# A Fourier mixing layer with a gated channel MLP: a chunk's two products exchanged in the middle of two passes, and the last chunks' loads and splits put elsewhere

## The chip, the cores and the metric

The kernel runs on one core of one Trainium2 chip. The metric is the device time of the whole program in microseconds (us), the median of several runs. TensorE (PE in the profile) multiplies; its weight loads are shown apart, as PEld. VectorE (DVE) and ScalarE (ACT) do elementwise work, GpSimd (POOL) and SyncE (SP) mostly issue DMAs here.

## The reference

`x` is 2048 x 512. It is layer-normalised to `xn`; `s` is the real part of a two-dimensional DFT of `xn`, written as matrix products; `g` is a channel MLP of `xn` behind SiLU.

```python
a = jnp.einsum("bsd,ed->bse", x, dft_hid_re)
b = jnp.einsum("bsd,ed->bse", x, dft_hid_im)
y = jnp.einsum("ts,bse->bte", dft_seq_re, a) - jnp.einsum("ts,bse->bte", dft_seq_im, b)
...
y = _layernorm(x, axis=-1)
h = _gelu(jnp.einsum("bsd,df->bsf", y, w1) + b1)
return jnp.einsum("bsf,fd->bsd", h, w2) + b2
...
xn = _layernorm(x, axis=-1)
s = _A_ref(xn, A_dft_seq_re, A_dft_seq_im, A_dft_hid_re, A_dft_hid_im)
g = _silu(_B_ref(xn, B_w1, B_b1, B_w2, B_b2))
return x + s * g
```

## The kernel before

All products keep float32 accuracy by splitting each operand into a high and a low half: ScalarE rounds it (`h` in the names, L64), VectorE subtracts the rounded value (`l`, L65). A product is then three matmuls, high by high, high by low, low by high. Seven products replace eight in each of the three large matrix multiplications.

The stages follow each other on TensorE: the hidden DFT (accumulators `pd`), the MLP's first half (`hx`, `hy`, `hz`), its second half (`ma`, `mb`), and then the sequence DFT, which the change touches. That one runs over 16 chunks `n` of 128 rows of the 2048 x 2048 matrices `ct`, each 128 x 1024 (512 KB), in passes `q`, listed in `passes`:

- Pass 0 multiplies `s4` (accumulators `px`) and `s3` (`pz`).
- Pass 1 multiplies `s2` (`pz`) and `a1` (`px`).
- Pass 2 goes on in the same accumulators with `b2` (`pz`) and `b1` (`px`); chunks 8 to 11 (`DEFER`) do only `b2`.
- Pass 3 multiplies `s1` (`pw`). Its last four chunks (`LAST`) are done in four *pieces* of 12 matmuls, one for each half of columns (`tau`) and of rows (`k`), so that the results can be finished piece by piece. Pieces 1 and 3 share the accumulator tile `pw30`, pieces 2 and 4 `pw31`.
- Pass 4 does the deferred `b1` of chunks 8 to 11, also in four pieces, into `px`.

In a product the chunk's split operand (`R_..h`, `R_..l`) is multiplied with a split left operand (`L_nh`, `L_nl`), which serves two chunks. `multiply_by` issues for each half of rows and columns (lh, rh), (lh, rl), (ll, rh): the second matmul is the first to need the chunk's low half, the third the first to need the left operand's. A product of a chunk has 12 matmuls.

A *unit* is one chunk of one pass. `ahead("load")`, `ahead("sum")` and `ahead("split")` run a few units ahead of the products, and their calls set the order on every queue: nothing is reordered later. `unit_load` issues the loads on SP; `unit_sum` forms the sums (L786, L791, L797); `unit_split` splits the left operand and the chunk. In pass 2 `unit_sum` splits `b1` first, then adds the held sum `t` to the raw chunk to make `b2` (L791), and `unit_split` splits that. At the end of a pass `evacuate` (L690) lets ScalarE copy the accumulators.

Places: the pool `op` has 39 places of 512 KB tiles for split operands, held sums and guests (`guest`); the pool `lp` (`room`) has 7 such places for raw loads. A load waits on SP until the place that it takes is free, and SP issues in order.

After each piece of pass 3, `end` issues on VectorE two multiplications with the gates (L999), which read the accumulator, and two additions (L1000), one of each for the two outputs that share `pw`, and SP stores the results (L1001). After a piece of pass 4 there is one of each; the addition reads `px`, a tile loaded at L964 with part of the input.

Of the kernel before, what the change touches and what calls it, by code (L numbers as in the profile page):

```python
# [22 lines left out]
def fnet_mixer_kernel(ctx: ExitStack, tc: tile.TileContext, x, xT, ct, wt, w1, w2, b1, b2, out):  # L23
# [3 lines left out]
    NS = S // P  # L27
# [7 lines left out]
    op = ctx.enter_context(tc.tile_pool(name="op", bufs=39))  # L35
# [6 lines left out]
    lp = early.enter_context(tc.tile_pool(name="lpa", bufs=4))  # L42
# [10 lines left out]
    def guest(name):  # L53
        return op.tile([P, 2, W], F32, tag="op", name=name)
# [4 lines left out]
    def room(name):  # L59
        return lp.tile([P, 2, W], F32, tag="l", name=name)  # L60
# [362 lines left out]
    for i in range(3, NS):  # L423
# [11 lines left out]
        if i == 4:  # L435
# [5 lines left out]
            lp = early.enter_context(tc.tile_pool(name="lpm", bufs=2, reuse_waits="tile"))  # L441
# [233 lines left out]
    def banks(name):  # L675
        return [acc_two(f"{name}{k}") for k in range(2)]

    def multiply_by(acc, left, right, first, last):
        (lh, ll), (rh, rl) = left, right
        for k in range(2):  # L680
            for tau in range(2):
                terms = [(lh[k], rh), (lh[k], rl), (ll[k], rh)]
                for i, (a, c) in enumerate(terms):
                    nc.tensor.matmul(acc[k][:, tau, :], a, c[:, tau, :], start=first and i == 0,  # L684
                                     stop=last and i == len(terms) - 1, skip_group_check=True)

    def evacuate(acc, name):
        out_ = [guest(f"{name}{k}") for k in range(2)]
        for k in range(2):
            nc.scalar.activation(out_[k], acc[k], AF.Copy)  # L690
        return out_
# [49 lines left out]
    def left(name, i):  # L741
        if name[0] == "s":
            return s_d[int(name[1]), i].rearrange("p (c e) -> p c e", c=2)
        e = int(name[1]) - 1
        return (a_d if name[0] == "a" else b_d)[i][:, :, e * W2:(e + 1) * W2].rearrange("c p e -> p c e")

    passes = [("s4", "s3"), ("s2", "a1"), ("b2", "b1"), ("s1",), ("b1",)]
    DEFER = (8, 9, 10, 11)  # L750
    units = [(q, n) for q in range(4) for n in range(NS)] + [(4, n) for n in DEFER]
    c_raw, c_left, c_ops, t_hold = {}, {}, {}, {}

    def names(q, n):
        return ("b2",) if q == 2 and n in DEFER else passes[q]

    at = {"load": 0, "sum": 0, "split": 0}

    def c_in(key, src, where):
        t = (guest if where == "op" else room)(f"{key}")  # L760
        nc.sync.dma_start(out=t, in_=src)
        return t

    def unit_load(u):
        q, n = units[u]
        if n % 2 == 0:
            t = room(f"la{q}_{n}")
            for v, name in enumerate(names(q, n)):
                nc.sync.dma_start(out=t[:, v, :].rearrange("p (c e) -> p c e", c=2), in_=left(name, n // 2))
            c_left[q, n // 2] = t  # L770
        if q == 0:
            c_raw[u] = {"s4": c_in(f"c22_{n}", ct[1, 1, n], "lp")}
            t_hold[n] = c_in(f"c12_{n}", ct[0, 1, n], "op")
        elif q == 1:
            c_raw[u] = {"a1": c_in(f"c11_{n}", ct[0, 0, n], "lp")}
        elif q in (2, 4):
            c_raw[u] = {"b1": c_in(f"c21_{q}_{n}", ct[1, 0, n], "lp")}
        elif n % 2:
            c_raw[u] = {"s1": c_in(f"d22_{n}", ct[1, 1, n], "lp")}

# [36 lines left out]
    def ahead(what, until):  # L817
        while at[what] < min(len(units), until):
            {"load": unit_load, "sum": unit_sum, "split": unit_split}[what](at[what])
            at[what] += 1  # L820
# [40 lines left out]
    for u, (p, j) in enumerate(m_units):  # L861
# [3 lines left out]
        if u == 1:  # L865

            n = NJ - 1
            h_product(n, 4)
            early.close()
            lp = early.enter_context(tc.tile_pool(name="lp", bufs=7, reuse_waits="tile"))  # L870
            gp = early.enter_context(tc.tile_pool(name="gp", bufs=4, reuse_waits="tile"))
            m_at["room"] = 1
        n = NJ - 1
# [9 lines left out]
        q = m_order.index(p)  # L883
# [23 lines left out]
    def factors(u, name):  # L907
        q, n = units[u]
        lr = [[t[:, (n % 2) * W2 + k * P:(n % 2) * W2 + (k + 1) * P] for k in range(2)] for t in c_left[q, n // 2][name]]
        return lr, c_ops[u][name]  # L910
# [7 lines left out]
    def gate_load(e, h):  # L918
        for k in range(2):
            gate[e, h, k] = gp.tile([P, 2, W], F32, tag="g", name=f"zr{e}{h}{k}") if h else guest(f"zr{e}{h}{k}")  # L920
            nc.sync.dma_start(out=gate[e, h, k], in_=z_d[h, 2 * e + k])

    def gate_open(e, h):
        for k in range(2):
            nc.scalar.activation(gate[e, h, k], gate[e, h, k], AF.Silu, bias=b2_t[:, 2 * e + k:2 * e + k + 1])

    def gated(e, h, k, src, dst):
        nc.vector.tensor_mul(dst, src, gate[e, h, k])
        nc.gpsimd.dma_start(out=dst, in_=xT[2 * h:2 * h + 2, 2 * e + k].rearrange("b p w -> p b w"), accum_op=ALU.add)

    def put_out(e, h, k, src):
        kk = 2 * e + k
        nc.gpsimd.dma_start(out=out[kk * P:(kk + 1) * P, 2 * h * W:2 * (h + 1) * W],
                            in_=src.rearrange("p b w -> p (b w)"))
# [8 lines left out]
    def after(q, n):  # L943
        for k in range(2):
            if (q, n) == (2, 1 + k):
                nc.vector.tensor_add(part["3", k], part["3", k], part["1", k])
                nc.vector.tensor_add(part["7", k], part["7", k], part["1", k])
            if (q, n) == (2, 3 + 2 * k):
                nc.vector.tensor_add(part["3", k], part["3", k], part["6", k])
            if (q, n) == (2, 4 + 2 * k):  # L950
                nc.vector.tensor_add(part["6", k], part["6", k], part["7", k])
            if (q, n) == (2, 8 + k):
                gated(0, 1, k, part["3", k], part["3", k])
            if (q, n) == (2, 10 + k):
                gated(1, 1, k, part["6", k], part["6", k])
            if (q, n) == (3, 1):
                nc.vector.tensor_add(part["7", k], part["7", k], part["8", k])
            if (q, n) == (3, 5):
                gated(1, 0, k, part["7", k], part["7", k])
            if (q, n) == (3, 8):  # L960
                put_out(1, 0, k, part["7", k])
            if (q, n) == (3, 9):
                part["x", k] = guest(f"px{k}")
                nc.sync.dma_start(out=part["x", k], in_=xT[0:2, k].rearrange("b p w -> p b w"))  # L964
        if (q, n) in GATES:
            gate_load(*GATES[q, n])
        if (q, n - 3) in GATES:
            gate_open(*GATES[q, n - 3])

    for u, (q, n) in enumerate(units):  # L970
        lead = 6 if q > 2 else 1 if q == 1 and n > 13 or q == 2 and n < 4 else 2
        ahead("load", u + lead + 4)
        ahead("sum", u + lead + 2)
        ahead("split", u + lead + 1)
        if n == 0:
            for name in passes[q] if q != 2 else ():
                acc[KEY[name]] = banks(f"p{KEY[name]}{q}")
        if q < 3 or q == 3 and n < NS - LAST:
            for name in names(q, n):
                multiply_by(acc[KEY[name]], *factors(u, name), n == 0 and q != 2, n == NS - 1 and name not in ("s2", "a1", "b1"))  # L980
                if n == NS - 1 and name in COPY:
                    for k, t in enumerate(evacuate(acc[KEY[name]], "p" + COPY[name])):
                        part[COPY[name], k] = t
        if u == 0:
            m_after(7)
        after(q, n)
# [3 lines left out]
    def piece(name, us, tau, k):  # L990
        for u in us:
            (lh, ll), (rh, rl) = factors(u, name)
            for i, (a, c) in enumerate([(lh, rh), (lh, rl), (ll, rh)]):
                nc.tensor.matmul(acc[KEY[name]][k][:, tau, :], a[k], c[:, tau, :], start=False,  # L994
                                 stop=u == us[-1] and i == 2, skip_group_check=True)
# [8 lines left out]
    for tau in range(2):  # L1004
        for k in range(2):
            piece("s1", [4 * NS - LAST + i for i in range(LAST)], tau, k)
            for do in zip(end(0, 1, k, tau, "w", "3"), end(1, 1, k, tau, "w", "6")):
                for o in do:
                    o()
    for tau in range(2):  # L1010
        for k in range(2):
            piece("b1", range(4 * NS, len(units)), tau, k)
            for o in end(0, 0, k, tau, "x", "x"):
                o()
# [33 lines left out]
```

## Time and profile before

| | |
|---|---|
| median of 3 runs | 680.47 us (680.40 to 682.38) |
| profiled execution, its time | 683.88 us |
| profiled execution, its span | 682.1 us |
| mean granted TensorE clock | 0.996 |
| VectorE busy | 538.3 us |
| DMA over the span | 171.49 MB, mean 251 GB/s |

The span is the time from the first to the last instruction. In the views, a group or row names the line, the engine, the operation and output<-inputs; a time in square brackets is idle time of the engine just before, with what ended it. The timeline has the start and the length of each instruction, with x for how many were joined. A table by stage has, for each stretch, the busy time of each engine with its count of instructions, then PEclk, the clock that TensorE was granted (1.00 is full), the busy share of the DMA engines, and GB/s. Matmuls overlap: a row of 0.39 us is followed by the next start 0.23 us later.

### The profile page before, as it was taken

How to read it: one execution, taken by the hardware profiler on the slowest of the kernel's cores; microseconds unless marked ns; L12 is line 12 of the kernel's file. 1: busy time of each engine (PE TensorE's matmuls, PEld its weight loads, DVE VectorE, ACT ScalarE, POOL GpSimd, SP SyncE). 2: the span in 40 equal slices, each digit the busy share in tenths (PEclk: the TensorE clock that was granted, in tenths of full speed). 3: DMA queues.
4: the chain of work that ended last, by engine and by line, in shares of the span. 5: the costliest groups of instructions: out<-in, count | busy, mean ns of one | idle time of the engine just before them, and what ended most of it. 6: DMA issues, size and time to landing. Idle time of an engine off the chain costs nothing.

```text
span 682.1 us, 8179 instructions
## 1 busy us (share of the span) xinstructions
PE 668.9 (98%) x2933; PEld 548.3 (80%) x2933; DVE 538.3 (79%) x595; ACT 347.8 (51%) x366; POOL 47.0 (7%) x80
## 2 busy tenths in 40 slices
PE   8999999999999999999999999999999999999986
PEld 5888888888888888888888888888888877888865
DVE  6877887877777864788979998649686399999975
ACT  4443566544545665555455554364456544637720
POOL 1000000212122100000000000000000000210100
PEclk9999999999999999999999999999999999999989
DMA  8666731899989997688799996325455279996953
GB/s 295 217 233 225 266 136 57 301 345 326 331 323 326 417 374 301 227 311 278 263 387 407 364 327 231 117 80 185 155 189 151 67 194 250 289 296 219 266 209 124
DMA packets 69897, 171.49 MB, mean 251 GB/s; under 512 B 6593, under 2 KB 20961, under 8 KB 69857
## 3 DMA queue, kind: packets, MB, share of 16 engines
q1 hardware_dynamic: 58304, 132.67, 55.9%
q0 software_dynamic: 11200, 37.76, 17.3%
q10 hardware_dynamic: 352, 0.54, 0.3%
q8 instruction: 23, 0.38, 0.2%
q14 instruction: 18, 0.14, 0.1%
HBM read 120.60 MB, written 50.35 MB: 251 GB/s over the span
## 4 chain that ended last, share of the span: by engine, by line
PE 92%; DMA 3%; DVE 3%; issue 1%; ACT 0%; SPq 0%; DVEq 0%; ACTq 0%
PE pz L684 18%; PE px L684 16%; PE pd L305 12%; PE ma L684 11%; PE hy L518 11%; PE mb L684 8%; PE hz L518 6%; PE pw L684 4%; PE hx L518 3%; DMA c<-ct 2%; PE px L994 2%; DMA rw<-wt 1%; PE pw L994 1%; DVE R_b2l L65 1%; DVE W L279 0%
## 5 line engine op out<-in xcount | busy, mean ns | idle before, releaser
L786 DVE TENSOR_TENSOR c<-c,c 128x1024 f32<-128x1024 f32 x32 | 39.0, 1218 | 3.5 <-DMA c<-ct 3.5
L65 DVE TENSOR_TENSOR w1l<-w1r,w1h 128x1792 fp32r<-128x1792 f32 x7 | 14.2, 2025 | 24.5 <-ACT w1h L64 24.5
L65 DVE TENSOR_TENSOR R_b1l<-c,R_b1h 128x1024 fp32r<-128x1024 f32 x16 | 19.4, 1220 | 16.8 <-ACT R_b1h L64 16.8
L305 PE MATMUL pd<-W,xt_0h 128*128 128x512 f32 x96 | 29.8, 392 | 0.0
L64 ACT ACTIVATE R_b2h<-c 128x1024 fp32r<-128x1024 f32 x16 | 17.0, 1060 | 25.1 <-DVE c L791 20.0
L684 PE MATMUL pw<-R_s1h,L 128*128 128x512 f32 x96 | 29.7, 389 | 0.0
L305 PE MATMUL pd<-W,xt_1h 128*128 128x512 f32 x96 | 29.6, 389 | 0.0
L64 ACT ACTIVATE R_s3h<-c 128x1024 fp32r<-128x1024 f32 x16 | 17.0, 1061 | 24.4 <-DVE c L786 16.1
L65 DVE TENSOR_TENSOR R_a1l<-c,R_a1h 128x1024 fp32r<-128x1024 f32 x16 | 19.6, 1222 | 10.3 <-PE px L684 8.0
L523 ACT ACTIVATE hc<-hc,b_t 128x1024 f32<-128x1024 f32 x14 | 16.2, 1154 | 20.3 <-DVE hc L558 19.7
L64 ACT ACTIVATE R_s2h<-c 128x1024 fp32r<-128x1024 f32 x16 | 16.9, 1059 | 16.9 <-PE px L684 15.2
L65 DVE TENSOR_TENSOR R_s2l<-c,R_s2h 128x1024 fp32r<-128x1024 f32 x16 | 19.5, 1221 | 5.4 <-PE pz L684 5.0
L64 ACT ACTIVATE R_b1h<-c 128x1024 fp32r<-128x1024 f32 x16 | 16.7, 1053 | 12.7 <-DMA c<-ct 8.7
L64 ACT ACTIVATE R_a1h<-c 128x1024 fp32r<-128x1024 f32 x16 | 16.9, 1056 | 12.3 <-PE pz L684 8.7
L65 DVE TENSOR_TENSOR R_s3l<-c,R_s3h 128x1024 fp32r<-128x1024 f32 x16 | 19.5, 1218 | 3.8 <-PE pz L684 3.8
L64 ACT ACTIVATE R_s1h<-c 128x1024 fp32r<-128x1024 f32 x16 | 16.4, 1052 | 11.3 <-DVE c L797 11.3
L684 PEld LDWEIGHTS pw<-R_s1h,L 128*128 128x128 f32 x96 | 18.0, 188 | 3.8
L305 PEld LDWEIGHTS pd<-W,xt_1h 128*128 128x128 f32 x96 | 18.0, 188 | 3.8
L305 PEld LDWEIGHTS pd<-W,xt_0h 128*128 128x128 f32 x96 | 17.8, 188 | 4.0
L794 POOL DMA_DIRECT2D c<-ct x8 | 6.9, 868 | 203.2 <-ACT R_a1h L64 144.8
L791 DVE TENSOR_TENSOR c<-c,c 128x1024 f32<-128x1024 f32 x16 | 19.6, 1223 | 0.4
L65 DVE TENSOR_TENSOR R_s4l<-c,R_s4h 128x1024 fp32r<-128x1024 f32 x16 | 19.5, 1217 | 0.4 <-PE px L684 0.4
(886 smaller groups left out, 2177.1 us busy)
## 6 DMA issues: line engine op xcount, KB each, us to landing
c<-ct SPq DMA_DIRECT2D x68, 512.0 KB, 5.9
m<-h_d SPq DMA_DIRECT2D x48, 512.0 KB, 6.6
h_d<-ht POOLq DMA_DIRECT2D x21, 512.0 KB, 7.2
s_d<-sa SPq DMA_DIRECT2D x32, 256.0 KB, 4.0
la<-s_d SPq DMA_DIRECT2D x32, 256.0 KB, 6.0
h_d<-hc POOLq DMA_DIRECT2D x13, 512.0 KB, 3.8
x<-x SPq DMA_DIRECT2D x16, 256.0 KB, 5.4
xT<-xT SPq DMA_DIRECT2D x8, 512.0 KB, 7.0
```

The costliest lines, as they stand in the source:

```text
L64: nc.scalar.activation(hi, src, AF.Copy)
L65: nc.vector.tensor_sub(lo, src, hi.bitcast(F32))
L305: nc.tensor.matmul(acc, xt[i, k][px], weights[m * NK + k][pw], start=n == 0, stop=n == len(terms) - 1)
L518: nc.tensor.matmul(acc[:, tau, :], w[:, W1_AT[p], k * P:(k + 1) * P], r[:, k, :], start=p in (1, 5, 2) and i == 0, stop=p in (2, 3, 4) and ...
L523: nc.scalar.activation(dst, src, AF.Gelu_apprx_tanh, bias=b1_t[:, row:row + 1])
L684: nc.tensor.matmul(acc[k][:, tau, :], a, c[:, tau, :], start=first and i == 0, stop=last and i == len(terms) - 1, skip_group_check=True)
L786: nc.vector.tensor_sub(t, t, raw)
L791: nc.vector.tensor_add(raw, raw, t)
L794: nc.gpsimd.dma_start(out=t, in_=ct[1, 1, n], accum_op=ALU.add)
L994: nc.tensor.matmul(acc[KEY[name]][k][:, tau, :], a[k], c[:, tau, :], start=False, stop=u == us[-1] and i == 2, skip_group_check=True)
```

## The change

Nothing is added to or taken from the computation: the same products, sums, splits, loads and stores are issued. Four things move.

1. `passes` names the two products of passes 1 and 2 the other way round, so that the product on `px` comes first in the middle of both passes. `in_order` turns them back for chunk 0 of pass 1 and chunk 15 of pass 2. The splits and the halves of the left operand follow `names`, so they are turned in all of pass 1.
2. The raw chunks of pass 4 (`c_4_8` to `c_4_11`) are loaded into places of `op` instead of `lp`.
3. `px` is loaded at chunk 12 of pass 3 instead of chunk 9.
4. The splits of the last two units (chunks 10 and 11 of pass 4, with their left operand) are issued after the `end` of pass 3's first piece, and not before the pieces.

```diff
-    passes = [("s4", "s3"), ("s2", "a1"), ("b2", "b1"), ("s1",), ("b1",)]
+    passes = [("s4", "s3"), ("a1", "s2"), ("b1", "b2"), ("s1",), ("b1",)]
...
+    def in_order(q, n):
+        return names(q, n)[::-1 if (q, n) in ((1, 0), (2, NS - 1)) else 1]
...
         elif q in (2, 4):
-            c_raw[u] = {"b1": c_in(f"c21_{q}_{n}", ct[1, 0, n], "lp")}
+            c_raw[u] = {"b1": c_in(f"c21_{q}_{n}", ct[1, 0, n], "lp" if q == 2 else "op")}
...
-            if (q, n) == (3, 9):
+            if (q, n) == (3, 12):
                 part["x", k] = guest(f"px{k}")
...
-        ahead("split", u + lead + 1)
+        ahead("split", min(u + lead + 1, 4 * NS + 2))
         if n == 0:
-            for name in passes[q] if q != 2 else ():
+            for name in in_order(q, n) if q != 2 else ():
                 acc[KEY[name]] = banks(f"p{KEY[name]}{q}")
         if q < 3 or q == 3 and n < NS - LAST:
-            for name in names(q, n):
+            for name in in_order(q, n):
...
             for do in zip(end(0, 1, k, tau, "w", "3"), end(1, 1, k, tau, "w", "6")):
                 for o in do:
                     o()
+            ahead("split", len(units))
```

TensorE in pass 2, where chunk 4 ends and chunk 5 begins, before:

```order
L684 MATMUL px_3812<-R_4_b1h,L_4h 128x512
L684 MATMUL px_3812<-R_4_b1l,L_4h 128x512
L684 MATMUL px_3812<-R_4_b1h,L_4l 128x512
L684 MATMUL pz_3809<-R_5_b2h,L_4h 128x512
L684 MATMUL pz_3809<-R_5_b2l,L_4h 128x512
L684 MATMUL pz_3809<-R_5_b2h,L_4l 128x512
```

The same place in the changed program:

```order
L684 MATMUL pz_3810<-R_4_b2h,L_4h 128x512
L684 MATMUL pz_3810<-R_4_b2l,L_4h 128x512
L684 MATMUL pz_3810<-R_4_b2h,L_4l 128x512
L684 MATMUL px_3811<-R_5_b1h,L_4h 128x512
L684 MATMUL px_3811<-R_5_b1l,L_4h 128x512
L684 MATMUL px_3811<-R_5_b1h,L_4l 128x512
```

Chunk 5 now begins with `b1`, and `b2` comes as the second product of its chunk.

VectorE at the pieces of pass 3, before (`R_8` to `R_11` here are the chunks of pass 4, `zr` the gates, `pw_5032` and `pw_5033` the two accumulators):

```order
L65 TENSOR_TENSOR R_9_b1l<-c_4_9_5202,R_9_b1h 128x1024
L65 TENSOR_TENSOR L_10_5289<-la_10_5226,L_10_5289 128x512
L65 TENSOR_TENSOR R_10_b1l<-c_4_10_5228,R_10_b1h 128x1024
L65 TENSOR_TENSOR R_11_b1l<-c_4_11_5252,R_11_b1h 128x1024
L999 TENSOR_TENSOR zr_4222<-pw_5032,zr_4222 128x512
L999 TENSOR_TENSOR zr_4634<-pw_5032,zr_4634 128x512
L1000 TENSOR_TENSOR zr_4222<-zr_4222,p_3774 128x512
L1000 TENSOR_TENSOR zr_4634<-zr_4634,p_4399 128x512
L999 TENSOR_TENSOR zr_4224<-pw_5033,zr_4224 128x512
L999 TENSOR_TENSOR zr_4636<-pw_5033,zr_4636 128x512
```

The same place in the changed program, whose lines 1003 and 1004 are 999 and 1000 of before:

```order
L65 TENSOR_TENSOR R_9_b1l<-c_4_9_5202,R_9_b1h 128x1024
L1003 TENSOR_TENSOR zr_4222<-pw_5032,zr_4222 128x512
L1003 TENSOR_TENSOR zr_4634<-pw_5032,zr_4634 128x512
L1004 TENSOR_TENSOR zr_4222<-zr_4222,p_3774 128x512
L1004 TENSOR_TENSOR zr_4634<-zr_4634,p_4415 128x512
L65 TENSOR_TENSOR L_10_5307<-la_10_5226,L_10_5307 128x512
L65 TENSOR_TENSOR R_10_b1l<-c_4_10_5228,R_10_b1h 128x1024
L65 TENSOR_TENSOR R_11_b1l<-c_4_11_5248,R_11_b1h 128x1024
L1003 TENSOR_TENSOR zr_4224<-pw_5033,zr_4224 128x512
L1003 TENSOR_TENSOR zr_4636<-pw_5033,zr_4636 128x512
```

The three splits moved from ahead of the first piece's four operations to behind them, ahead of the second piece's.

SP's queue, from the first load of pass 4's chunks to the last one, before:

```order
L761 DMA c_4_8_5184<-ct 128x1024
L761 DMA c_4_9_5202<-ct 128x1024
L769 DMA la_10_5226<-b_d_135 128x2x256
L761 DMA c_4_10_5228<-ct 128x1024
L964 DMA px_5246<-xT 128x2x512
L964 DMA px_5248<-xT 128x2x512
L761 DMA c_4_11_5252<-ct 128x1024
```

The same stretch in the changed program:

```order
L765 DMA c_4_8_5184<-ct 128x1024
L765 DMA c_4_9_5202<-ct 128x1024
L773 DMA la_10_5226<-b_d_135 128x2x256
L765 DMA c_4_10_5228<-ct 128x1024
L765 DMA c_4_11_5248<-ct 128x1024
L968 DMA px_5285<-xT 128x2x512
L968 DMA px_5287<-xT 128x2x512
```

The last chunk's load now stands ahead of both `px` loads. What each load waits for also differs: before, `c_4_11` took the place in `lp` that the sum of chunk 15 of pass 3 (L797) frees; now it takes a place in `op` that the products of chunk 7 of pass 3 free, and the second `px` one that those of chunk 9 free.

## The prediction

> **What bounds the kernel now.** I read the page's busy shares first, then who waits for whom on TensorE's weight loads (which stop first when an operand is late), then stages.
>
> ```profile
> PE 668.9 (98%) x2933; PEld 548.3 (80%) x2933; DVE 538.3 (79%) x595; ACT 347.8 (51%) x366; POOL 47.0 (7%) x80
> ...
> PEld pw L994 <- DVE zr L999: 3.6, 1, 3.6
> PEld pz L684 <- DVE R_b2l L65: 3.4, 3, 1.7
> ...
> 538.00:617.00 79.00, 76.86 (x337) 62.66 (x336) 74.06 (x66) 40.57 (x42) 10.87 (x11) 1.00 0.84 230
> 617.00:650.00 33.00, 33.00 (x147) 27.36 (x146) 31.47 (x31) 23.66 (x29) 3.59 (x4) 1.00 0.84 259
> 650.00:682.10 32.10, 23.70 (x97) 18.77 (x95) 18.63 (x28) 1.44 (x2) 0.00 (x0) 0.92 0.41 152
> ```
>
> TensorE is the bound; in the stages that the change touches it waits for these two alone, 4 times, and an edit that removes no matmul can win no more. Both are waits for VectorE, and VectorE is itself nearly full there: 74.06 of 79 us in pass 2 (538 to 617) and 31.47 of 33 in pass 3. So what TensorE gains, VectorE must be able to follow.
>
> To size the waits I need the pace of matmuls without any. The chain in order of time has 60 in one piece, then the starts that matter:
>
> ```profile
> 584.74 13.60 PE pz L684 x60
> ...
> 538.01 0.39 PE L684 MATMUL pz<-R_b2h,L_0h 128*128 128x512 f32 x1
> ...
> 561.29 0.50 PE L684 MATMUL pz<-R_b2l,L_4h 128*128 128x512 f32 x1 [0.77 <-DVE R_b2l L65]
> ...
> 568.35 0.50 PE L684 MATMUL pz<-R_b2l,L_4h 128*128 128x512 f32 x1 [1.32 <-DVE R_b2l L65]
> ...
> 617.22 0.39 PE L684 MATMUL pw<-R_s1h,L 128*128 128x512 f32 x1
> ...
> 649.86 0.39 PE L994 MATMUL pw<-R_s1h,L 128*128 128x512 f32 x1
> ...
> 655.07 0.39 PE L994 MATMUL pw<-R_s1h,L 128*128 128x512 f32 x1
> 658.63 0.50 PE L994 MATMUL pw<-R_s1h,L 128*128 128x512 f32 x1 [3.17 <-DVE zr L999]
> ...
> 665.84 0.39 PE L994 MATMUL px<-R_b1h,L 128*128 128x512 f32 x1
> ...
> 676.49 0.39 PE L994 MATMUL px<-R_b1h,L 128*128 128x512 f32 x1
> ```
>
> 13.60/60 is 0.2267 us a matmul, 2.72 a product of 12. Pass 2 has 28 products (12 chunks of two, 4 of one): 76.16 us, and it took 617.22 - 538.01 = 79.21. **Pass 2 loses 3.05.** In the tail, the matmul after 655.07 was due at 655.30 and came at 658.63: 3.33 idle. The next 24 matmuls took 665.84 - 658.63 = 7.21 instead of 5.44: 1.77 more. **The tail loses 5.10.** The 1.77 is a slower clock (column PEclk, before DMA share and GB/s):
>
> ```profile
> 658.60:659.90 1.30, 1.27 (x6) 1.05 (x6) 1.30 (x3) 0.00 (x0) 0.00 (x0) 1.00 0.00 0
> 659.90:663.30 3.40, 3.40 (x10) 2.63 (x9) 2.47 (x5) 0.00 (x0) 0.00 (x0) 0.50 0.70 251
> 663.30:666.00 2.70, 2.70 (x13) 2.24 (x12) 2.30 (x4) 0.00 (x0) 0.00 (x0) 1.00 0.30 94
> 568.40:570.00 1.60, 1.60 (x7) 1.34 (x8) 1.60 (x2) 0.46 (x1) 0.00 (x0) 1.00 0.99 207
> ```
>
> After 3.33 us idle the granted clock is 0.50 for 3.4 us; after the idle at 568.35 (1.3 to 1.7 us) it stays 1.00. The Trainium skill, TensorE: Matmul & The Clock Gate, section "Part 1: The HAM clock gate (the "warmup" mystery)", says the array falls to half rate after an idle window of about 3.4 us, that the window runs freely, and that a busy window restores it; these rows agree.
>
> **The turned products in pass 2.** No instruction is added. Of a chunk, b1 is split first and b2 = c21 + held sum later; before, b2 was multiplied first. The change gives b2l one product, 2.72 us, more, and asks for the left operand's low half (third matmul) at the same chunk start as before. VectorE's order stays, and from 540.22 it runs without a gap through these rows, so its times stay and TensorE moves against them:
>
> ```profile
> 540.22 1.23 DVE L65 TENSOR_TENSOR R_b1l<-c,R_b1h 128x1024 fp32r<-128x1024 f32 x1 [10.69 <-ACT R_b1h L64]
> ...
> 558.89 1.22 DVE L65 TENSOR_TENSOR L_4l<-la,L_4h 128x1024 fp32r<-128x1024 f32 x1
> 560.02 1.22 DVE L65 TENSOR_TENSOR R_b2l<-c,R_b2h 128x1024 fp32r<-128x1024 f32 x1
> ...
> 567.08 1.22 DVE L65 TENSOR_TENSOR R_b2l<-c,R_b2h 128x1024 fp32r<-128x1024 f32 x1
> ...
> 592.38 1.22 DVE L65 TENSOR_TENSOR L_12l<-la,L_12h 128x1024 fp32r<-128x1024 f32 x1
> ```
>
> Walking TensorE at 5.44 a chunk from 538.01, with 0.05 from VectorE's end to the matmul (568.30 to 568.35):
> - Chunk 4 starts at 559.77; its third matmul, at 560.22, needs L_4l, there at 558.89 + 1.22 + 0.05 = 560.16. It clears by 0.06. Its b2l (560.02) is needed at 562.7.
> - Chunk 5's second product starts at 567.93, its second matmul at 568.16; R_b2l is there at 567.08 + 1.22 + 0.05 = 568.35. Wait 0.19.
> - Chunk 12 starts at 538.01 + 8 x 5.44 + 4 x 2.72 + 0.19 = 592.60; its third matmul, at 593.05, needs L_12l, there at 593.65. Wait 0.60: what is late next is the left operand, which the turn doesn't help.
>
> So 3.05 - 0.79 = **2.26 gained**. Bounds: 0, where VectorE slips by as much, and 3.05.
>
> **The turned products in pass 1, and the boundaries: nothing.** Pass 1 has no TensorE wait. Its first chunk still multiplies s2 first but splits it second, one VectorE operation (1.14) later; VectorE has finished and idles:
>
> ```profile
> 432.67 1.22 DVE L65 TENSOR_TENSOR R_s2l<-c,R_s2h 128x1024 fp32r<-128x1024 f32 x1
> ...
> 453.18 1.23 DVE L65 TENSOR_TENSOR L_2l<-la,L_2h 128x1024 fp32r<-128x1024 f32 x1 [10.68 <-ACT L_2h L64]
> ```
>
> That operand, ready near 435, is used at the pass's start, 87 us before 538.01, at about 451. The chunks turned at pass ends keep ScalarE's copies of one accumulator under the other's 2.72 us product, as now; so VectorE's catch-up still begins at 540.22. Without that cover a boundary would wait about a product's length.
>
> **The tail: loads and splits.** The last c21 load now waits for a loading place, behind px on SP; its landing sets everything after:
>
> ```profile
> 640.44 1.70 SPq L964 DMA_DIRECT2D px<-xT  x2
> 643.28 0.34 SPq L761 DMA_DIRECT2D c<-ct  x1
> ...
> DMA to landing us min/median/max: 6.4/7.0/11.7
> ...
> 655.06 1.06 ACT L64 ACTIVATE R_b1h<-c 128x1024 fp32r<-128x1024 f32 x1 [4.68 <-DMA c<-ct]
> ...
> 647.99 2.36 DVE L65 TENSOR_TENSOR R_b1l<-c,R_b1h 128x1024 fp32r<-128x1024 f32 x2 [0.26 <-ACT R_b1h L64]
> 650.27 0.68 DVE L65 TENSOR_TENSOR L<-la,L 128x512 fp32r<-128x512 f32 x1
> 650.88 1.22 DVE L65 TENSOR_TENSOR R_b1l<-c,R_b1h 128x1024 fp32r<-128x1024 f32 x1
> 656.15 1.23 DVE L65 TENSOR_TENSOR R_b1l<-c,R_b1h 128x1024 fp32r<-128x1024 f32 x1 [4.06 <-ACT R_b1h L64]
> 657.30 1.28 DVE L999 TENSOR_TENSOR zr<-pw,zr 128x512 f32<-128x512 f32 x2
> 658.50 1.28 DVE L1000 TENSOR_TENSOR zr<-zr,p 128x512 f32<-128x512 f32 x2
> 659.70 1.28 DVE L999 TENSOR_TENSOR zr<-pw,zr 128x512 f32<-128x512 f32 x2
> ```
>
> The third last piece rewrites the accumulator that L999 reads, and L999 stands behind that split. With the change the load takes the operand place that pass 3's chunk 7 frees. Pass 3 now starts at 617.22 - 2.26 = 614.96, so chunk 7 ends at 614.96 + 8 x 2.72 = 636.7, before px in SP's queue. Landing 6.4 to 11.7 later is 643 to 648.5; ScalarE can round it by 651.5. The four waiting chunks hold operand places longer, but the splits that take places next wait for chunks that end by 644.8, and ScalarE reaches them later. px goes out last, when chunk 9 frees a place (642.2); at its landing time of 11.2 us
>
> ```profile
> DMA to landing us min/median/max: 11.2/11.2/11.2
> ```
>
> it is there near 653.4, and its first reader comes near 664.
>
> Now the pieces. The first starts at 649.86 - 2.26 = 647.60 and ends at 647.60 + 2.72 + 0.16 = 650.48 (a matmul's 0.39 runs 0.16 past the next start). VectorE has done chunk 9's split at 650.35, starts L999 at 650.52, and its two L999 end at 651.80. The third piece, due at 653.04, doesn't wait. But behind the first piece's four operations now stand three splits, ahead of the second piece's L999, **which the fourth piece waits for**: 650.52 + 1.20 + 1.20 (pairs, steps of the rows above) + 0.61 + 1.14 + 1.14 + 1.28 = 657.09. The fourth piece, due at 655.76, starts at 657.14: a new wait of 1.38. Behind it TensorE holds only the four last px pieces, which follow without a wait: 657.14 + 5 x 2.72 + 0.16 = 670.90, against 676.88 now. Bounds of this added wait: 0, if the splits fit into VectorE's idle time, and 3.33, the wait it replaces. I take 1.38, whose parts all have rows; at this length the clock stayed up.
>
> **Sum.** 676.88 - 670.90 = 5.98: 2.26 from pass 2, 3.33 - 1.38 = 1.95 from idle, 1.77 from the clock. What follows the last matmul stays. Against the profiled execution's 683.88 (span 682.1 and 1.78 around it) that makes 677.9. The timed median, 680.47, is 3.41 below that execution, and two of three runs lie 1.9 below the third (682.38), about the 1.77 of the slow clock. The idle of 3.33 halved the clock and that at 568.35 did not, so a slightly shorter idle may keep it. I take the median to pay the idle but not the clock: 680.47 - 2.26 - 1.95 = **676.3**.
>
> **Rivals.**
> 1. *The median pays the half clock too* (659.90 to 663.30 speaks for it): all 5.98 go, 674.5. By the rule of the Trainium skill, TensorE: Matmul & The Clock Gate, Part 1, a free-running window decides whether such an idle time halves the clock, so it may differ from run to run; no row here shows the window's phase.
> 2. *VectorE is the bound in pass 2*: it slips with TensorE and the waits move from R_b2l to L_4l, R_b2l and L_12l whole. For it: 0.06 us of room at chunk 4. Against: its row times don't come from TensorE. Only the tail's 1.95 is left: 678.5.
> 3. *The split's move does nothing*: in a timed run the late load lands before 651.6, no piece waits now, and the change only adds its 1.38: 680.47 - 2.26 + 1.38 = 679.6. For it: 3.41 us between the executions; against: landing would have to shrink from 11.7 to 8.3.
> 4. *Slower*: the last load in its operand place lands so late that its split, ahead of the second piece's L999, holds the fourth piece. That piece starts 1.06 + 1.15 + 1.28 = 3.5 after landing. To lose 2.04 the end must pass 675.11 + 2.04 (676.88 less 1.77), so the piece must start after 663.4 and the load land after 659.9, 23 us from issue. At 660 it gives 682.6. The slowest here took 11.7.
>
> **Chances.** This measurement tells 0.3%, 2.04 us, from no change. Forecast 0.46, first rival 0.31, second 0.08, third 0.10, fourth 0.05. Faster by over 0.3% (below 678.43): forecast, first, and part of the second, 0.80. Within: 0.15. Slower: 0.05. The range takes the first rival with pass 2's upper bound (680.47 - 5.98 - 0.79 = 673.7) and reaches past the second: 673.6 to 679.2; it leaves out the fourth and most of the third.
>
> **What would show it.** In the changed profile: no wait of pz for R_b2l above 0.3 us, one near 0.6 for L_12l; pass 3 starting near 615.0; the last c21 load issued before px, near 637; one TensorE wait of about 1.4 before the fourth piece, on L1003 (was L999), with the clock at 1.00 after it. Wrong would be a wait for L_4l or of pass 1, or a fourth-piece wait above 3 us with the clock at 0.50.

## The result, and the profile after

| | before | changed |
|---|---|---|
| median | 682.38 us (680.40 to 684.34, 5 runs) | 677.55 us (676.91 to 677.84, 5 runs) |
| profiled execution, time and span | 683.88 us, 682.1 us | 676.92 us, 675.1 us |
| mean granted TensorE clock | 0.996 | 0.999 |

The ratio of the times is 0.9932 (95% interval 0.9906 to 0.9958): the changed kernel is faster by 0.7%. The kernel before was run twice more than in the table at the start; its median over five runs is 1.9 us above that over the first three, which matters below.

The page of the changed kernel, busy time of each engine:

```profile
PE 666.7 (99%) x2933; PEld 547.2 (81%) x2933; DVE 537.8 (80%) x595; ACT 347.4 (51%) x366; POOL 47.0 (7%) x80
```

The waits of its weight loads on TensorE from pass 2 on (total, times, longest):

```profile
PEld pw L998 <- DVE zr L1003: 1.6, 1, 1.6
PEld px L684 <- DVE L_12l L65: 0.7, 1, 0.7
PEld pz L684 <- DVE R_b2l L65: 0.4, 1, 0.4
PEld px L684 <- DVE L_4l L65: 0.2, 1, 0.2
```

The table by stage, for pass 2 and for pass 3 up to the last pieces:

```profile
536.70:613.80 77.10, 76.80 (x337) 62.84 (x336) 72.14 (x64) 40.59 (x43) 10.87 (x11) 1.00 0.87 234
613.80:646.40 32.60, 32.60 (x145) 27.03 (x144) 31.20 (x31) 21.34 (x25) 3.02 (x3) 1.00 0.81 264
```

The two old groups of waits (3.6 and 3.4 us) have become four single ones (2.9 us in all). VectorE did not get lighter: it still works 72.1 of 77.1 us in pass 2 and 31.2 of 32.6 in pass 3. Its own rows in pass 2 stand where they stood, 1.29 us earlier like the pass itself (567.08 and 592.38 before, pass 2 from 538.01; now from 536.72):

```profile
565.79 1.22 DVE L65 TENSOR_TENSOR R_b2l<-c,R_b2h 128x1024 fp32r<-128x1024 f32 x1
...
591.09 1.22 DVE L65 TENSOR_TENSOR L_12l<-la,L_12h 128x1024 fp32r<-128x1024 f32 x1
```

The rows of TensorE in the changed kernel that answer to those of before (start, length, operation, idle time just before and what ended it):

```profile
536.72 0.39 PE L684 MATMUL px<-R_b1h,L_0h 128*128 128x512 f32 x1
...
566.69 0.39 PE L684 MATMUL pz<-R_b2h,L_4h 128*128 128x512 f32 x1
567.06 0.50 PE L684 MATMUL pz<-R_b2l,L_4h 128*128 128x512 f32 x1
567.40 0.40 PE L684 MATMUL pz<-R_b2h,L_4l 128*128 128x512 f32 x1
...
591.67 0.39 PE L684 MATMUL px<-R_b1l,L_12h 128*128 128x512 f32 x1
592.36 0.50 PE L684 MATMUL px<-R_b1h,L_12l 128*128 128x512 f32 x1 [0.30 <-DVE L_12l L65]
...
613.80 0.39 PE L684 MATMUL pw<-R_s1h,L 128*128 128x512 f32 x1
...
646.44 0.39 PE L998 MATMUL pw<-R_s1h,L 128*128 128x512 f32 x1
...
654.38 0.39 PE L998 MATMUL pw<-R_s1h,L 128*128 128x512 f32 x1
655.98 0.50 PE L998 MATMUL pw<-R_s1h,L 128*128 128x512 f32 x1 [1.22 <-DVE zr L1003]
...
669.53 0.39 PE L998 MATMUL px<-R_b1h,L 128*128 128x512 f32 x1
```

Two measures are read from such rows for every kernel below. **Pass 2's loss** is the time from its first matmul to pass 3's first, less 28 products of 2.72 us: 613.80 - 536.72 - 76.16 = 0.92 us, against 3.05 before. **The tail's loss** is the time from the first piece's first matmul to the last one's start, less 95 steps of 0.2267 us (21.54): 669.53 - 646.44 - 21.54 = 1.55 us, against 5.10 before. Together they fell by 5.68 us. The two profiled executions differ by 6.96; the other 1.29 is that pass 2 began at 536.72 instead of 538.01. That isn't the change's: in the twelve profiles below pass 2 begins between 537.53 and 538.47, whatever was edited, and the three further executions of the changed kernel have 537.64, 537.92 and 538.47.

VectorE, SP and ScalarE of the changed kernel at the pieces:

```profile
649.36 1.29 DVE L1003 TENSOR_TENSOR zr<-pw,zr 128x512 f32<-128x512 f32 x2 [0.39 <-PE pw L998]
650.57 1.28 DVE L1004 TENSOR_TENSOR zr<-zr,p 128x512 f32<-128x512 f32 x2
651.77 0.69 DVE L65 TENSOR_TENSOR L<-la,L 128x512 fp32r<-128x512 f32 x1
652.37 2.36 DVE L65 TENSOR_TENSOR R_b1l<-c,R_b1h 128x1024 fp32r<-128x1024 f32 x2
654.64 1.28 DVE L1003 TENSOR_TENSOR zr<-pw,zr 128x512 f32<-128x512 f32 x2
...
633.36 2.50 SPq L765 DMA_DIRECT2D c<-ct  x2
639.63 1.71 SPq L968 DMA_DIRECT2D px<-xT  x2
...
647.96 1.99 ACT L64 ACTIVATE R_b1h<-c 128x1024 fp32r<-128x1024 f32 x2
```

The last loads of c21 are issued before `px`, and ScalarE rounds the two last chunks in one stretch at 647.96, where before it waited for a DMA and began the last one at 655.06. The four operations of the first piece now stand ahead of the last three splits, and the second piece's L1003 behind them: the fourth piece waits for that. This is the layout that the prediction walked through. The clock stays up behind that wait (PEclk 1.00):

```profile
655.90:669.90 14.00, 13.92 (x60) 11.19 (x60) 10.08 (x17) 0.00 (x0) 0.00 (x0) 1.00 0.45 161
```

### The profile page after: what moved, and what is told of

Same layout as the page of the kernel before. It is cut to its first block, busy times and chain, and to the rows that moved or that the text cites. A ratio compares the mean times of both kernels' runs of the same rounds, so it can differ in the third digit from the quotient of the medians.

```text
span 675.1 us, 8181 instructions
## 1 busy us (share of the span) xinstructions
PE 666.7 (99%) x2933; PEld 547.2 (81%) x2933; DVE 537.8 (80%) x595; ACT 347.4 (51%) x366; POOL 47.0 (7%) x80
## 4 chain that ended last, share of the span: by engine, by line
PE 81%; DVE 7%; issue 7%; DMA 4%; POOL 0%; SPq 0%; DVEq 0%; POOLq 0%
PE px L684 14%; PE pz L684 13%; PE pd L305 12%; PE hy L518 11%; PE ma L684 11%; PE mb L684 8%; PE hz L518 6%; PE hx L518 3%; DVE R_b2l L65 2%; PE px L998 2%; DMA rw<-wt 1%; DMA p<-xT 1%; DVE R_b1l L65 1%; DMA out<-p 1%; DMA zr<-z_d 1%
## 5 line engine op out<-in xcount | busy, mean ns | idle before, releaser
L64 ACT ACTIVATE R_s2h<-c 128x1024 fp32r<-128x1024 f32 x16 | 16.9, 1056 | 12.4 <-PE px L684 10.5
L64 ACT ACTIVATE R_s1h<-c 128x1024 fp32r<-128x1024 f32 x16 | 16.4, 1052 | 11.7 <-DVE c L801 11.7
L64 ACT ACTIVATE w2h<-w 128x1024 fp32r<-128x1024 f32 (+1 forms) x14 | 13.2, 946 | 12.7 <-DVE w L623 3.9
```

Of the source, the lines that this page charges most:

```text
L64: nc.scalar.activation(hi, src, AF.Copy)
```

## The experiments

Each table row gives the two losses of the profiled execution, and the times of one comparison; kernels with the same letter ran on the same chip beside the same runs of the kernel before (A: median 683.03 us, 23 runs; B: 682.56, 11 runs; C: 682.60, 11 runs).

| kernel | pass 2 loses | tail loses | median (range), us | ratio to before, 95% interval |
|---|---|---|---|---|
| A: turn alone | 0.96 | 6.33 | 682.76 (680.84 to 684.66) | 1.0005 (0.9991 to 1.0019) |
| A: tail alone | 3.05 | 1.50 | 680.26 (679.33 to 681.11) | 0.9967 (0.9953 to 0.9981) |
| A: splits not moved | 0.97 | 1.12 | 678.09 (677.53 to 678.30) | 0.9938 (0.9916 to 0.9959) |
| A: changed again | 0.96 | 1.50 | 677.86 (677.50 to 678.08) | 0.9935 (0.9915 to 0.9954) |
| B: splits moved, load late | 0.90 | 1.80 | 678.36 (677.79 to 678.87) | 0.9938 (0.9922 to 0.9954) |
| B: splits behind second piece | 0.95 | 0.26 | 676.88 (676.46 to 677.10) | 0.9916 (0.9901 to 0.9931) |
| B: and later sums in pass 2 | 0.00 | 0.26 | 675.81 (675.15 to 676.92) | 0.9903 (0.9886 to 0.9920) |
| B: changed again | 0.90 | 1.50 | 678.03 (677.51 to 678.18) | 0.9932 (0.9915 to 0.9949) |
| C: pass 1 not turned | 0.92 | 1.50 | 678.50 (677.35 to 680.04) | 0.9946 (0.9929 to 0.9963) |
| C: turned everywhere | 0.96 | 1.58 | 678.23 (677.61 to 678.55) | 0.9941 (0.9925 to 0.9957) |
| C: changed again | 0.92 | 1.51 | 678.08 (677.81 to 678.63) | 0.9942 (0.9926 to 0.9957) |

None of them leaves out a part of the computation.

### The turn of the products alone

Loads, `px` and splits stay as before the change:

```diff
-            c_raw[u] = {"b1": c_in(f"c21_{q}_{n}", ct[1, 0, n], "lp" if q == 2 else "op")}
+            c_raw[u] = {"b1": c_in(f"c21_{q}_{n}", ct[1, 0, n], "lp")}
-            if (q, n) == (3, 12):
+            if (q, n) == (3, 9):
-        ahead("split", min(u + lead + 1, 4 * NS + 2))
+        ahead("split", u + lead + 1)
-            ahead("split", len(units))
```

> Only the two products are turned; loads, px and splits stand as before. Theory (TensorE runs 2.1 us ahead in pass 2 but VectorE and the last c21 load keep their times, so the tail's idle time grows by what pass 2 gives): pass 2 loses about 0.9 us in place of 3.05, the idle time before the third last piece grows from 3.3 to about 5.4 us, the clock falls after it, and the time is within 1 us of before. Rival (the gains simply add): the idle time stays at 3.3 and the time is 2.1 us below before.

Measured: no difference in time (0.9991 to 1.0019), although pass 2 lost 0.96 us in place of 3.05. The timeline of ScalarE, VectorE and TensorE of this kernel at the third piece:

```profile
654.29 1.06 ACT L64 ACTIVATE R_b1h<-c 128x1024 fp32r<-128x1024 f32 x1 [4.11 <-DMA c<-ct]
...
655.38 1.23 DVE L65 TENSOR_TENSOR R_b1l<-c,R_b1h 128x1024 fp32r<-128x1024 f32 x1 [3.49 <-ACT R_b1h L64]
656.52 1.28 DVE L1003 TENSOR_TENSOR zr<-pw,zr 128x512 f32<-128x512 f32 x2
...
657.85 0.79 PE L998 MATMUL pw<-R_s1h,L 128*128 128x512 f32 x1 [4.62 <-DVE zr L1003]
```

Its table by stage just behind (the clock follows the five busy times):

```profile
658.50:660.20 1.70, 1.70 (x6) 1.31 (x5) 1.70 (x4) 0.00 (x0) 0.00 (x0) 0.50 0.55 204
```

The last c21 load and the sum whose place it takes:

```profile
641.83 1.22 DVE L801 TENSOR_TENSOR c<-c,d 128x1024 f32<-128x1024 f32 x1
...
643.07 0.34 SPq L765 DMA_DIRECT2D c<-ct  x1
```

TensorE reached its first piece at 647.64, 2.22 us before the 649.86 of the kernel before, and then waited for the same event: the late load's landing, 654.29 against 655.06 by ScalarE's row. The load went out as soon as VectorE's sum had ended, 105.2 us behind pass 2's first matmul; before it was 105.3 (643.28 - 538.01). It doesn't move with TensorE. It took 11.1 us to land, against 11.7. The third piece could start at 657.85 against 658.63. So 0.8 of the 2.2 us got through in this execution, most of it by the faster landing, and the idle time grew from 3.17 to 4.62 (about 5.4 was expected), with the clock at 0.50 behind it as before. A gain ahead of an event that has its own time is turned into waiting for it.

### The tail alone

Loads, `px` and splits as in the change, the products in the order of before:

```diff
-    passes = [("s4", "s3"), ("a1", "s2"), ("b1", "b2"), ("s1",), ("b1",)]
+    passes = [("s4", "s3"), ("s2", "a1"), ("b2", "b1"), ("s1",), ("b1",)]
-        return names(q, n)[::-1 if (q, n) in ((1, 0), (2, NS - 1)) else 1]
+        return names(q, n)
```

> Only the tail is changed (c21 into operand places, px at chunk 12, late splits); the products stand as before. Theory: pass 2 loses 3.05 us as before, the third piece does not wait, the fourth waits about 1.4 us, the clock stays up; 3.5 to 3.7 us below before in the profile. If timed runs of before also pay the half clock, the timed difference is 3.5, otherwise about 2.0. Rival (the gains need each other also this way round): less than 1 us.

Measured: 0.9967 (0.9953 to 0.9981), 2.8 us between the medians, with pass 2 at its old loss of 3.05 and the tail at 1.50, 3.6 us less than before, as expected; the timed 2.8 lies between the two values that were expected, 2.0 and 3.5. In times against the median of 683.03: the turn alone 0.3 us, the tail alone 2.8, both 5.2. The parts don't add up because the tail is the lock on the turn.

### Load early, splits where they were

```diff
-        ahead("split", min(u + lead + 1, 4 * NS + 2))
+        ahead("split", u + lead + 1)
-            ahead("split", len(units))
```

> The changed kernel with its turned products and its loads, but all splits ahead of the pieces as before. Theory (the earlier load does it, the split's place only chooses which piece waits): the third piece waits about 1.4 us for the first piece's L1003 and the fourth does not wait; within 0.5 us of the changed kernel. Rival (the split's move is what frees the pieces): 2 us or more above the changed kernel.

Measured: 678.09 us beside 677.86 for the changed kernel, whose ranges overlap. VectorE and TensorE of this kernel:

```profile
650.80 2.35 DVE L65 TENSOR_TENSOR R_b1l<-c,R_b1h 128x1024 fp32r<-128x1024 f32 x2
653.07 1.28 DVE L1003 TENSOR_TENSOR zr<-pw,zr 128x512 f32<-128x512 f32 x2
...
654.41 0.50 PE L998 MATMUL pw<-R_s1h,L 128*128 128x512 f32 x1 [0.80 <-DVE zr L1003]
```

With both last chunks there, the splits run in one stretch, and the first piece's L1003 comes at 653.07: now the third piece waits, 0.80 us (about 1.4 was expected), where in the changed kernel the fourth does, 1.22. **With the load early, moving the splits is worth nothing**; in the profile it costs 0.4 us.

> The changed kernel once more, as the measure for the others of this call: 4 to 5 us below before, fourth piece waiting about 1.2 us, pass 2 losing about 0.9 us. In its profile the start of pass 2 tells how much the stages ahead of the change vary: 536.7 us in its first profile, 538.0 in that of before.

Measured: 677.86 us; the fourth piece waits 1.22 us on TensorE (1.6 in its weight load), as in the first profile of the changed kernel.

### Splits moved, load late

The opposite half: loads and `px` as before the change, turn and splits as changed.

```diff
-            c_raw[u] = {"b1": c_in(f"c21_{q}_{n}", ct[1, 0, n], "lp" if q == 2 else "op")}
+            c_raw[u] = {"b1": c_in(f"c21_{q}_{n}", ct[1, 0, n], "lp")}
-            if (q, n) == (3, 12):
+            if (q, n) == (3, 9):
```

> The changed kernel, but the late loads of c21 and the load of px stand where they stood before the change (places of the ring lp, px after chunk 9); the turn of the products and the last splits behind the first last piece stay. Theory (either half of the tail's edit is nearly enough, as the kernel with the load alone already showed): the late load lands so that ScalarE's second R_b1h and with it VectorE's second R_b1l come near 655.4, as in the profile with the turn alone, but now the first piece's L1003 and L1004 stand ahead of it. The second piece's L1003 then begins near 656.5 in place of 655.6, so that the fourth piece waits about 2.2 us in place of 1.2 and the third does not wait; the clock stays 1.00. Time about 1.0 us above the changed kernel, some 3.8 us below the kernel before. Rival A (the loads carry all of the gain): the wait is 4 us or more, the clock falls to 0.50 behind it, and the time is 4 us or more above the changed kernel, at the kernel before. Rival B: the load comes earlier for another reason (px no longer matters), and the time is that of the changed kernel.

Measured: 678.36 us beside 678.03, ranges overlapping, tail loss 1.80.

```profile
653.70 1.06 ACT L64 ACTIVATE R_b1h<-c 128x1024 fp32r<-128x1024 f32 x1 [3.44 <-DMA c<-ct]
...
654.80 1.23 DVE L65 TENSOR_TENSOR R_b1l<-c,R_b1h 128x1024 fp32r<-128x1024 f32 x1 [0.21 <-ACT R_b1h L64]
655.94 1.28 DVE L1003 TENSOR_TENSOR zr<-pw,zr 128x512 f32<-128x512 f32 x2
...
657.27 0.50 PE L998 MATMUL pw<-R_s1h,L 128*128 128x512 f32 x1 [1.51 <-DVE zr L1003]
```

The mechanism was as expected (no wait of the third piece, a longer one of the fourth, clock up), the size not: the load landed 0.6 us earlier than in the profile on which the expectation was built, so the wait is 1.51 and not 2.2. ScalarE still waits 3.44 us for the late load; VectorE uses that time for the first piece. So **either half of the tail's edit takes most of the old wait away**, and the second adds nothing to the first. The half called the load is itself two edits, the place in `op` and `px` later. Before, the load went out at 643.28, as the sum that frees its place ended, so it is the place that held back its issue; what `px`, on its way at the same time, added to the 10.5 to 11.7 us of landing in the kernels with the late load (6.5 to 7.4 in the changed kernel) was not tested apart.

### Splits one piece later

```diff
-            ahead("split", len(units))
+            if k:
+                ahead("split", len(units))
```

> The changed kernel with the last splits one last piece later, behind the second piece's end and not the first's. Theory: the changed kernel's one wait left in the tail (the fourth piece on VectorE's L1003 of the second piece, 1.2 us on PE and 1.6 in its weight load) is the price of the splits' 3.0 us standing ahead of that L1003. Behind it they delay no piece of pw (the third and fourth pieces read banks that are then free), and px's first piece finds its last R_b1l near 658.5 only as its last three matmuls come. No wait of the pieces over 0.3 us, time 1.2 to 1.5 us below the changed kernel. Rival: the wait moves to px's first piece or to the last L1003, which end the kernel through VectorE and the store of the output, and the time is that of the changed kernel within 0.4 us.

Measured: 676.88 us (676.46 to 677.10) beside 678.03 (677.51 to 678.18): the ranges are apart, 1.15 between the medians (1.2 to 1.5 was expected). All waits of its weight loads from pass 2 on:

```profile
PEld px L684 <- DVE L_12l L65: 0.7, 1, 0.7
PEld pz L684 <- DVE R_b2l L65: 0.4, 1, 0.4
PEld px L998 <- DVE zr L1003: 0.4, 1, 0.4
PEld px L684 <- DVE L_4l L65: 0.2, 1, 0.2
```

The wait of the fourth piece is gone, a `px` piece waits 0.4 us instead (0.3 was the most expected), and the tail loses 0.26 in place of 1.50. The wait of the fourth was the price of the three splits ahead of the second piece's L1003, which the prediction had named.

### And pass 2's sums later

In addition, the sums and gated products of pass 2 stand four chunks later in VectorE's queue:

```diff
-            if (q, n) == (2, 1 + k):
+            if (q, n) == (2, 5 + k):
-            if (q, n) == (2, 3 + 2 * k):
+            if (q, n) == (2, 7 + 2 * k):
-            if (q, n) == (2, 4 + 2 * k):
+            if (q, n) == (2, 8 + 2 * k):
-            if (q, n) == (2, 8 + k):
+            if (q, n) == (2, 12 + k):
-            if (q, n) == (2, 10 + k):
+            if (q, n) == (2, 14 + k):
```

> As the kernel with the splits behind the second piece, and pass 2's sums of products and gated products (lines 950 to 959) stand four chunks later in their order. Theory: the changed kernel's three waits left in pass 2 (L_4l 0.2, R_b2l of chunk 5 0.4, L_12l 0.7 us) are the price of these sums standing ahead of the splits in VectorE's queue, where it has no idle time from 538.9 to 610 us. Four chunks later they come when VectorE has caught up: the three waits are gone, pass 2's loss falls from 0.9 us to under 0.2, and the time is another 0.7 to 1.0 us lower. Rival: VectorE stays saturated to the end of pass 2, the same work in all, and the wait comes at a later chunk's R_b2l or at pass 3's first R_s1l: no gain, or a loss of up to 1 us.

Measured: no wait in pass 2 is left, and its loss is 0.00. The median is 675.81, 1.07 lower; the ranges overlap (675.15 to 676.92), so the profile's 0.95 is the better measure. From pass 2 on, one wait is left in the whole program:

```profile
PEld px L998 <- DVE zr L1003: 0.4, 1, 0.4
```

This is the fastest version here: 0.9903 of the time before (0.9886 to 0.9920).

> The changed kernel once more, as the measure for the three others on this chip: 677.5 to 678.1 us, the fourth piece's wait 1.2 to 1.6 us, 0.9 us lost in pass 2.

Measured: 678.03 us, losses 0.90 and 1.50.

### Pass 1 not turned, and everything turned

The first takes pass 1's turn out, the second also turns the two chunks that the change leaves:

```diff
-    passes = [("s4", "s3"), ("a1", "s2"), ("b1", "b2"), ("s1",), ("b1",)]
+    passes = [("s4", "s3"), ("s2", "a1"), ("b1", "b2"), ("s1",), ("b1",)]
-        return names(q, n)[::-1 if (q, n) in ((1, 0), (2, NS - 1)) else 1]
+        return names(q, n)[::-1 if (q, n) in ((2, NS - 1),) else 1]
```

```diff
-        return names(q, n)[::-1 if (q, n) in ((1, 0), (2, NS - 1)) else 1]
+        return names(q, n)[::-1 if (q, n) in () else 1]
```

> The changed kernel with pass 1 in the order of before (s2 before a1 in every chunk), so that the copies of px at its end no longer lie under a product of pz before pass 2's first product b1 accumulates into px. Theory one, as the prediction put it: without that cover the boundary waits about a product's length, 2.7 us, and the time is up to 2.7 us above the changed kernel. Theory two, from the changed kernel's copies (L690, 1.03 us each, the first 1.1 us and the second 0.2 us after the pass's end is reached by the half that they read): each half of px is copied while the other half is still multiplied, and the wait before pass 2 is at most 0.3 us; the time is that of the changed kernel within 0.4 us, and pass 1's turn is worth nothing by itself. Lost in pass 2 0.9 us in either case, since VectorE begins its catch-up 2.2 us behind pass 1's last matmul in both orders.

> The changed kernel with the turn in every chunk: b1 before b2 in pass 2's last chunk too, and a1 before s2 in pass 1's first. Theory: the last product of pass 2 is then pz's, ScalarE's two copies of pz (609.98 and 611.28 us in the changed profile) come 2.7 us later, and with them its roundings for pass 3; VectorE's idle time of 1.8 and 0.9 us just there, waiting for a DMA, takes up most of it, but the rest, up to 1 us, is found again as a longer wait of the fourth last piece, since VectorE has next to no idle time from 615 to 646 us. Time 0 to 1.0 us above the changed kernel. Rival: it is lost whole, 2.7 us above. Pass 1's first chunk: nothing, as its operand is ready over 10 us before it is multiplied.

> The changed kernel once more, as the measure for the two others on this chip: 677.5 to 678.1 us, the fourth piece's wait 1.2 to 1.6 us, 0.9 us lost in pass 2.

Measured: 678.50, 678.23 and 678.08 us, all ranges overlapping. Without pass 1's turn, ScalarE's copies of `px` lie at the boundary of pass 2, and TensorE begins pass 2 behind the first of them (timeline):

```profile
537.25 1.03 ACT L690 ACTIVATE p<-px 128x1024 f32<-128x1024 f32 x1 [0.39 <-PE px L684]
538.55 1.03 ACT L690 ACTIVATE p<-px 128x1024 f32<-128x1024 f32 x1 [0.27 <-PE px L684]
...
538.35 0.48 PE L684 MATMUL px<-R_b1h,L_0h 128*128 128x512 f32 x1
```

The weight loads' wait there:

```profile
PEld px L684 <- ACT p L690: 0.2, 1, 0.2
```

The half of `px` that is multiplied first is copied while the other half is still multiplied; its copy ends at 538.28, and pass 2 starts at 538.35. The boundary costs 0.2 us in the weight load. Turned everywhere, the same 0.2 appears ahead of pass 3, and the tail loses 1.58. So of the turned products pass 2's alone matter, and the two exceptions at the ends are worth nothing that a timing can tell.

### The kernel before, a second execution

> The kernel before once more, for a second profiled execution of it. Theory: the executions of before differ by whether the idle time before the third last piece halves the clock. Either this one shows an idle time of 3.3 us or more and a mean clock of 0.993 to 0.996 with about 1.8 us lost at clock 0.50 behind it, at 682 to 684.7 us; or the load lands earlier, the idle time is under 3.2 us, the clock stays 1.00 (0.998 in the mean), and the execution takes 680.5 to 682 us. Rival: the times scatter for a reason ahead of pass 2, and the tail loses 5.1 us as before whatever the time. Pass 2 loses 3.05 us in either case.

Measured: 681.82 us, pass 2's loss 617.45 - 538.25 - 76.16 = 3.04. The weight loads' waits from pass 2 on:

```profile
PEld pz L684 <- DVE R_b2l L65: 3.4, 3, 1.7
PEld pw L994 <- DVE zr L999: 2.9, 1, 2.9
```

The third piece in the timeline:

```profile
658.15 0.50 PE L994 MATMUL pw<-R_s1h,L 128*128 128x512 f32 x1 [2.46 <-DVE zr L999]
```

The stage behind it:

```profile
658.00:663.00 5.00, 4.85 (x21) 4.00 (x22) 5.00 (x10) 0.00 (x0) 0.00 (x0) 1.00 0.52 184
```

The same wait, 0.7 us shorter (2.46 idle against 3.17; the load landed in 10.9 us against 11.7), leaves the clock at 1.00, and the tail loses 2.79 us instead of 5.10. The kernel before has **two kinds of executions**, with the half clock in the tail and without. Whether the load's landing alone decides between them, two profiles can't show; the last section has a second condition. The timed runs can only be sorted by their mean clock, 0.996 and 0.998 in the two profiles: of the 23 runs of comparison A, 7 have a mean clock of 0.998, with a median of 680.96 us, and 16 have 0.993 to 0.996, with a median of 683.21 us. That these 16 lost their clock in the tail is inferred: single runs of kernels without the long wait have 0.995 or 0.996 too (the slowest of the tail alone, of pass 1 not turned and of the later sums), and no profile shows where they lost it. The times also scatter within a kind: a further run of this kernel, beside this one, took 680.06 us at 0.998.

## Why the prediction was right, point by point

- **What bounds the kernel: right.** TensorE, held by VectorE at two places. With both places cleared (the splits one piece later and the sums later, on top of the change) the two losses went from 8.15 us to 0.26.
- **The turn in pass 2: right, a little too large.** Predicted 2.26, measured 3.05 - 0.92 = 2.13. VectorE kept its times, so the rival in which it slips with TensorE (678.5) is out. Of the waits, chunk 5's second matmul came 566.69 to 567.06, 0.14 late (predicted 0.19), and chunk 12's third 591.67 to 592.36, 0.46 late (predicted 0.60). What was missing from the sum is that the step behind each wait is slow too: 567.06 to 567.40 is 0.34, 0.11 over the pace. The prediction's sign of failure, a wait for L_4l, did show, at 0.2 us in the weight load, of which the matmuls lost 0.04 (558.93 to 559.20 in place of 0.23): the 0.06 of room was counted to the matmul, but the wait stands on its weight load, which began at 558.86 after 0.19 of waiting, ahead of the matmul.
- **Pass 1 and the boundaries: right that they are worth nothing; the reason was wrong.** "Without that cover a boundary would wait about a product's length" fell: without the cover it waits 0.2 us.
- **The tail: right.** Predicted: the first piece to wait is the fourth, on L1003, for 1.38 us; measured 1.37 late and 0.11 in the step behind it, tail loss 1.55. The clock stayed at 1.00 and the last c21 load went out before `px`, as predicted. What the prediction didn't see is that the two parts of the tail's edit are alternatives.
- **The sum in the profile: right.** Predicted 5.98 from the two places, measured 5.68.
- **From the profile to the median: the step that was off.** Predicted 676.3, measured 677.55. It took "the median to pay the idle but not the clock": an execution with an idle time of 3.33 us at full clock. No execution like that was profiled. The one at half clock loses 5.10 us in its tail; the one at full clock has the shorter wait as well and loses 2.79. For an execution like the second the gain is 2.13 + 2.79 - 1.50 = 3.42, not 4.21; 680.47, if it was of that kind, then gives 677.05. For one like the first it is 2.13 + 5.10 - 1.50 = 5.73. The timed runs, sorted by their clock, show about these sizes: 680.96 - 677.86 = 3.10 and 683.21 - 677.86 = 5.35. The measured 4.8 between the medians of the first comparison lies between them, so that the predicted 4.21 comes near it is in part luck; against the 680.47 from which the prediction subtracted, the gain is 2.9. In the larger sample most runs of the kernel before (16 of 23, by their clock) pay the half clock, as the first rival has it; its 674.5 failed all the same, since it took the whole 5.98 from a median that by its time hadn't paid it. What kind each of the three runs behind that median was isn't recorded.
- **The rival in which the split's move does nothing** named a true thing by another way: the move does add nothing, but because the earlier load has already done its work. **The slower rival** (the load in its operand place landing 23 us late) didn't occur: ScalarE rounds the last chunk by 649.95.

## What to carry to other kernels

A gain of time ahead of a late event only turns into more waiting for it: look for the next event that keeps its own time (here a load whose place comes free late) before pricing an edit, and price edits in pairs when one sits behind the other. In an in-order queue, put work that nobody waits for soon behind the work that the busiest engine waits for; here that alone was worth as much as the earlier load, and doing it one step further gave another 1.15 us. When a wait is of the length at which the clock falls in some executions and not in others, it has two prices, and a median of three runs doesn't say which one it shows.

## What the hardware did that was not expected

- An idle time of TensorE of 2.46 us left the granted clock at 1.00, one of 3.17 us was followed by 0.50, and so was one of 4.62. The Trainium skill, TensorE: Matmul & The Clock Gate, section "Part 1: The HAM clock gate (the "warmup" mystery)", has the clock fall after at least one idle window of about 3.4 us. Here it fell at 659.91, 1.28 us after TensorE had started again, so the 3.4 us before the fall were not without matmuls; on that point the prediction's "these rows agree" was too quick.
- The length of the idle time isn't the only condition that fits. In the kernel before, the clock came back at 663.32 and fell next at 680.39, behind the last matmul (0.73 in 680.30:680.50); in the turn alone the same three changes are at 657.54, 660.95 and 678.02. In both the distances are 3.41 and 17.07 us, one and five times 3.41, as if the clock were decided at steps of 3.41 us. In the second execution of before it fell only behind the last matmul, near 677.81; counted back in such steps, a step ended at 657.33, within the idle time. The step before each of the two moments, before and in the second execution:

```profile
656.50:659.90 3.40, 1.27 (x6) 1.05 (x6) 3.40 (x6) 0.00 (x0) 0.00 (x0) 1.00 0.00 0
```

```profile
653.92:657.33 3.41, 1.77 (x8) 1.13 (x6) 1.66 (x2) 1.06 (x1) 0.00 (x0) 1.00 0.17 67
```

TensorE was idle for 2.1 of 3.4 us in the first, and the clock fell; for 1.6 in the second, and it stayed. So where the steps lie may decide as well as how late the load lands, as the prediction's first rival allowed. That is worked out from three profiles and not tested.
- The runs of the kernel before fall into two groups by their mean clock, 0.998 against 0.993 to 0.996, 2.25 us apart in their medians. That is more than the 1.77 us that the half clock itself cost in the profile, which fits a longer wait coming together with the lower clock.
- A wait that ends in a weight load costs up to 0.1 us more than the idle time shows. At the waits of 0.4 us and more in the weight load the matmul takes 0.50 us in the record instead of 0.39, and the next follows after 0.34 instead of 0.23 (567.06 and 655.98 in the changed kernel); at its wait of 0.2 us, at 558.93, it takes 0.43 and the next follows after 0.27.
